# Attention gate columns by matmul, the other late modulation columns on VectorE in chunks two and three

## Chip, cores, metric

One core of one Trainium2 chip. The metric is the device time of one execution in microseconds (us); the profile's span is about 1.8 us shorter. The profile names the engines PE (TensorE matmuls), PEld (TensorE weight loads), DVE (VectorE), ACT (ScalarE), POOL (GpSimd) and SPq (the queue in which SyncE issues DMAs). Its `arena` tiles lie in SBUF and its `ps` tiles in PSUM, to which all matmuls write; an eviction is the copy of such a result from PSUM to SBUF. The granted clock is the share of TensorE's full clock that the throttle let through.

## The reference

An adaLN block: a modulation of six groups of 1024 columns, attention with 32 query heads over 512 cached keys, and a feed-forward part.

```python
mod = (silu(c) @ w_mod).reshape(1, 6, 1, 1024)        # w_mod: 1024 x 6144
sa, ca, ga, sb, cb, gb = mod[:, 0], ..., mod[:, 5]
h = layernorm(x) * (1 + ca) + sa                      # x: 2048 x 1024
x = x + ga * attention(h, k_cache, v_cache, wq, wo)
h = layernorm(x) * (1 + cb) + sb
x = x + gb * ((silu(h @ w_gate) * (h @ w_up)) @ w_down)
```

`sa` and `ca` are needed first. The attention gate `ga` is needed at the first output projection, and `sb, cb, gb` only in the feed-forward part.

## The kernel before

The 2048 rows run in four chunks of 512; I number them 0 to 3, so the title's "two and three" are chunks 1 and 2. A loop of steps `i` goes through 4 x 32 heads. A step issues, in this order, loads, the query projection of head `i+3`, the scores of head `i-1`, and the product with the values (`pv`) of head `i-2`. After the 32nd head of a chunk comes the output projection. One piece of background work (layer norm of a later chunk, or a "row task" that copies a column of gates onto all partitions) is issued at the end of each step. `finish(task)` issues all that is left of a task at once; I call this its forced end.

The early 16 columns of the modulation are made by matmuls before the loop. The other 32 (8 per group) are made one at a time: a transposing DMA brings 128 columns of `w_mod` into SBUF, and VectorE multiplies them with `silu(c)` and sums.

```python
def load_mt(n):                       # transposed load, issued by SyncE
    T.op(Q_mt[n % 2], lambda: SP.dma_start_transpose(mt[n % 2]..., w_mod[:, (NE + n) * P:(NE + n + 1) * P]), writes=[B_mt[n % 2]])

def mod_col(n):                       # the sum, VectorE
    T.op(DVE, lambda: V.scalar_tensor_tensor(mt[n % 2], mt[n % 2], 1.0, sc_row, op0=ALU.mult, op1=ALU.mult,
                                             accum_out=mcol[:, n:n + 1]), reads=[B_scr], writes=[B_mt[n % 2], B_mcol])

def row_task(dst, dbuf, src, sbuf):
    # cut: copies src to c6 on GpSimd
    def diags(n): ...                 # four GpSimd multiplications of ident by a column
    diags(0)
    yield
    for n in range(2):
        for q in range(4):
            mm(bank(XB, P, q * P), ones_bf, diag[q], ...)
        T.op(DVE, lambda: V.tensor_copy(dst[:, n * 512:(n + 1) * 512], bank(XB)), writes=[PB[XB], dbuf])
        if n == 0:
            diags(1)                  # must wait for the four matmuls above
        yield

LOADX = {2: 1, 19: 2, 40: 3}
LOADT = {(3 + 3 * n) if n < DT else (27 + (5 * (n - DT)) // 2): n for n in range(NL)}   # DT = 8, NL = 32
LOADO = {5 + (21 * p) // 8: p for p in range(8)}
for i in range(1, NA + 2):
    if i % 4 == 1:
        load_wq((i + 3) // 4 + 1)     # 1 MB of query weights, two buffers
    if i in LOADX: load_x(LOADX[i])
    if i in LOADT: load_mt(LOADT[i])
    if i - 4 in LOADT:
        mod_col(LOADT[i - 4])         # cut: at the end of a group mod_take, mod_gain or a row task in front of the list
    if i in LOADO: load_wo(LOADO[i])  # 1 MB of output weights
    if i == 8: add_ln1(1)             # cut: later chunks, add_ln2
    if i + LEAD < NA:
        if (i + LEAD) % Hq == 0: finish(ln1[(i + LEAD) // Hq])
        qproj(i + LEAD)               # 8 matmuls, then its eviction on VectorE
    # cut: scores(i - 1), pv(i - 2); pv ends with a reciprocal and a multiplication on VectorE
    # and a transposing DMA of the head; after the last head of a chunk: finish(rows), oproj(chunk)
    run_bg(1)
```

The softmax here doesn't subtract the row's maximum and nothing guards it: scores larger than these inputs give would overflow.

## Time and profile before

| | before |
|---|---|
| device time, median of 3 runs | 1281.27 us (1281.27 to 1281.44) |
| span of the profile | 1280.0 us |
| TensorE busy, VectorE busy | 99%, 38% |
| granted clock | 1.000 |
| transposed loads of `w_mod` in the loop | 32 |

From the profile's page of the kernel before, the engines and the two groups that matter. Columns of a group: line, engine, operation, tiles, shapes, count, then busy us, mean ns of one, and idle time before.

```profile
PE 1262.1 (99%) x7428; PEld 644.3 (50%) x7568; DVE 483.0 (38%) x889; ACT 339.4 (27%) x382; POOL 48.0 (4%) x102
...
L266 PE MATMUL ps<-arena 128*128 128x512 bf16 (+2 forms) x7251 | 1257.3, 333 | 11.5 <-DVE rl L639 1.7
...
L532 DVE SCALAR_TENSOR_TENSOR arena<-arena 128x1024 bf16<-128x1024 bf16 x32 | 38.6, 1206 | 0.4 <-DMA arena<-in_w_mod_dram 0.4
```

TensorE is full: only a wait of TensorE itself can be won. The sums (L532) take 38.6 us of an engine with much idle time, so their sum says nothing of their worth. One caution: this trace has 7251 matmuls of L266 where the trace of the changed kernel has 7391, and the two programs differ there only by the added one-column matmuls, which are another group. So records are missing, and the 11.5 us of idle time are mostly holes.

A better ruler is the start of the reciprocal (L639) that ends each head: there are 128, none missing. I call the time from reciprocal n-1 to reciprocal n "the interval at head n", counting from 0. Without a stall it is 3.50 us, and 58.75 us where a projection lies between (heads 32, 64, 96).

The timeline of VectorE in the kernel before, at head 23 (start us, duration us, engine, line, operation; in brackets the idle time before and what ended it):

```profile
113.87 0.18 DVE L639 RECIPROCAL rl<-ps 128x4 f32<-128x4 f32 x1 [1.08 <-PE ps L266]
...
117.04 0.69 DVE L578 CAST arena<-ps 128x512 bf16<-128x512 f32 x1
118.81 0.18 DVE L639 RECIPROCAL rl<-ps 128x4 f32<-128x4 f32 x1 [1.08 <-PE ps L266]
```

The interval is 118.81 - 113.87 = 4.94 us. Who waited, from the view of the waits of PE:

```profile
PE ps L266 <- DMA arena<-in_A_wq_dram: 1.5, 1, 1.5
```

TensorE waited 1.5 us, once, for query weights. Their DMA stands in SyncE's queue between transposes. From the timeline of SPq, where the duration is the time to issue:

```profile
104.82 1.73 SPq L645 DMA_TRANSPOSE arena<-arena  x1
106.66 0.53 SPq L338 DMA_DIRECT2D arena<-in_A_wq_dram  x1
107.23 4.78 SPq L527 DMA_TRANSPOSE arena<-in_w_mod_dram  x1
```

The second kind of stall is made by the order on VectorE. Its timeline at heads 65 and 66:

```profile
377.09 0.18 DVE L639 RECIPROCAL rl<-ps 128x4 f32<-128x4 f32 x1 [1.08 <-PE ps L266]
...
377.91 0.68 DVE L378 BATCH_NORM_STATS2 st<-x_res 128x6 f32<-128x512 bf16 x1
...
378.76 1.17 DVE L532 SCALAR_TENSOR_TENSOR arena<-arena 128x1024 bf16<-128x1024 bf16 x1
...
380.26 0.68 DVE L578 CAST arena<-ps 128x512 bf16<-128x512 f32 x1
380.86 0.17 DVE L639 RECIPROCAL rl<-ps 128x4 f32<-128x4 f32 x1
```

Normalisation, LN statistics and the sum all come before the eviction of the next query (L578), with no idle time between. The next projection needs that PSUM bank, and the interval becomes 3.77 us (380.86 - 377.09).

### The profile page before, as it was taken

How to read it: one execution, taken by the hardware profiler on the slowest of the kernel's cores; microseconds unless marked ns; L12 is line 12 of the kernel's file. 1: busy time of each engine (PE TensorE's matmuls, PEld its weight loads, DVE VectorE, ACT ScalarE, POOL GpSimd, SP SyncE). 2: the span in 40 equal slices, each digit the busy share in tenths (PEclk: the TensorE clock that was granted, in tenths of full speed). 3: DMA queues.
4: the chain of work that ended last, by engine and by line, in shares of the span. 5: the costliest groups of instructions: out<-in, count | busy, mean ns of one | idle time of the engine just before them, and what ended most of it. 6: DMA issues, size and time to landing. Idle time of an engine off the chain costs nothing.

```text
span 1280.0 us, 17545 instructions
## 1 busy us (share of the span) xinstructions
PE 1262.1 (99%) x7428; PEld 644.3 (50%) x7568; DVE 483.0 (38%) x889; ACT 339.4 (27%) x382; POOL 48.0 (4%) x102
## 2 busy tenths in 40 slices
PE   8999999999999999999999999999999999999999
PEld 4555545555445564455644444444444444444444
DVE  3576425764247652265322331233222331221222
ACT  3655303555025550055510111011100111011100
POOL 2110100000001010000000000000000000000000
PEclk9999999999999999999999999999999999999999
DMA  8899603867017741064352974046421654035200
GB/s 288 212 242 282 130 1 71 193 133 165 1 21 169 161 104 41 1 128 116 71 148 71 287 234 132 17 144 168 133 73 40 198 148 132 18 112 168 66 9 25
DMA packets 241133, 155.29 MB, mean 121 GB/s; under 512 B 137376, under 2 KB 228384, under 8 KB 241056
## 3 DMA queue, kind: packets, MB, share of 16 engines
q1 hardware_dynamic: 182816, 95.45, 31.6%
q10 hardware_dynamic: 58240, 58.72, 14.7%
q8 instruction: 59, 0.97, 0.3%
q14 instruction: 18, 0.15, 0.0%
HBM read 117.44 MB, written 4.19 MB: 95 GB/s over the span
## 4 chain that ended last, share of the span: by engine, by line
PE 96%; DMA 2%; DVE 1%; issue 1%; ACT 0%; SPq 0%
PE ps L266 96%; DMA arena<-arena 1%; DMA arena<-in_A_wq_dram 1%; DVE arena L532 0%; DVE arena L642 0%; PE ps L270 0%; DVE st L378 0%; DVE rl L639 0%; DMA c_row<-in_c_dram 0%; DVE arena L578 0%; ACT arena L621 0%; DVE mv L382 0%; DVE arena L455 0%; DVE tmp L661 0%; DVE arena L663 0%
## 5 line engine op out<-in xcount | busy, mean ns | idle before, releaser
L266 PE MATMUL ps<-arena 128*128 128x512 bf16 (+2 forms) x7251 | 1257.3, 333 | 11.5 <-DVE rl L639 1.7
L266 PEld LDWEIGHTS ps<-arena 128*128 128x128 bf16 x7391 | 637.2, 98 | 625.9 <-issue 4.2
L621 ACT ACTIVATE arena<-ps 128x1024 bf16<-128x1024 f32 x256 | 261.8, 1023 | 354.4 <-PE ps L266 342.6
L828 ACT ACTIVATE arena<-ps 128x512 bf16<-128x512 f32 x112 | 66.9, 597 | 507.0 <-PE ps L266 507.0
L829 DVE TENSOR_TENSOR arena<-ps,arena 128x512 bf16<-128x512 f32 x112 | 77.5, 692 | 276.2 <-PE ps L266 276.2
L661 DVE TENSOR_TENSOR tmp<-ps,rowb 128x512 f32<-128x512 f32 (+1 forms) x65 | 44.4, 683 | 319.6 <-PE ps L266 319.6
L578 DVE CAST arena<-ps 128x512 bf16<-128x512 f32 x124 | 85.6, 691 | 47.2 <-PE ps L266 47.1
L642 DVE TENSOR_TENSOR arena<-ps,rl 128x512 bf16<-128x512 f32 x128 | 88.5, 692 | 4.9 <-DVE rl L639 0.5
L639 DVE RECIPROCAL rl<-ps 128x4 f32<-128x4 f32 x128 | 23.4, 183 | 125.0 <-PE ps L266 124.8
L383 POOL TENSOR_SCALAR rstd<-mv 128x1 f32<-128x1 f32 x31 | 12.9, 416 | 879.7 <-DVE mv L382 879.7
L378 DVE BATCH_NORM_STATS2 st<-x_res 128x6 f32<-128x512 bf16 x62 | 42.3, 682 | 3.5 <-DMA x_res<-in_A_x_dram 3.5
L532 DVE SCALAR_TENSOR_TENSOR arena<-arena 128x1024 bf16<-128x1024 bf16 x32 | 38.6, 1206 | 0.4 <-DMA arena<-in_w_mod_dram 0.4
L663 DVE TENSOR_TENSOR arena<-tmp,x_res 128x512 bf16<-128x512 f32 (+1 forms) x33 | 22.3, 676 | 1.1
L663 DVE TENSOR_TENSOR x_res<-tmp,x_res 128x512 bf16<-128x512 f32 x32 | 22.2, 692 | 1.1
L394 DVE TENSOR_SCALAR arena<-arena,gain,mod_bf 128x512 bf16<-128x512 bf16 x56 | 20.4, 406 | 0.0
L385 POOL TENSOR_TENSOR rstd<-rstd,mhalf 128x1 f32<-128x1 f32 x31 | 17.6, 568 | 2.6
L389 DVE TENSOR_SCALAR nsc<-x_res,mv,rstd 128x1024 bf16<-128x1024 bf16 x30 | 16.1, 538 | 1.0 <-POOL rstd L385 1.0
L547 POOL TENSOR_SCALAR arena<-arena,c 128x128 bf16<-128x128 bf16 x24 | 14.4, 616 | 25.4 <-PE ps L266 25.1
L382 DVE BATCH_NORM_AGGREGATE mv<-st 128x2 f32<-128x12 f32 x31 | 6.5, 209 | 1.1
L266 PEld LDWEIGHTS ps<-sc_bf,arena 128*128 128x128 bf16 x128 | 4.4, 96 | 1.9
L459 ACT ACTIVATE arena<-ps,mod_bf,gain_f 128x512 bf16<-128x512 bf16 x3 | 2.2, 774 | 10.3 <-DVE arena L455 10.3
L266 PE MATMUL ps<-sc_bf,arena 128*128 128x1 bf16 x128 | 4.3, 163 | 0.0
(43 smaller groups left out, 33.7 us busy)
## 6 DMA issues: line engine op xcount, KB each, us to landing
arena<-in_A_wq_dram SPq DMA_DIRECT2D x31, 1024.0 KB, 5.8
arena<-in_B_w_gate_dram ACTq DMA_DIRECT2D x28, 1024.0 KB, 5.4
arena<-in_B_w_up_dram ACTq DMA_DIRECT2D x28, 1024.0 KB, 8.2
arena<-in_A_wo_dram SPq DMA_DIRECT2D x8, 1024.0 KB, 6.9
arena<-in_B_w_down_dram SPq DMA_DIRECT2D x7, 1024.0 KB, 8.5
arena<-in_w_mod_dram SPq DMA_DIRECT2D x8, 512.0 KB, 9.1
out_dram<-arena SPq DMA_DIRECT2D x15, 256.0 KB, 2.0
x_res<-in_A_x_dram SPq DMA_DIRECT2D x3, 1024.0 KB, 7.7
```

The costliest lines, as they stand in the source:

```text
L266: T.op(PE, lambda: TE.matmul(out_ap, lhsT, rhs, start=start, stop=stop, skip_group_check=skip), reads=reads, writes=[bank_buf])
L378: T.op(DVE, lambda: V.bn_stats(st_[sl][:, hf * 6:hf * 6 + 6], x_res[:, t, hf * 512:hf * 512 + 512]), reads=[B_x[t]], writes=[B_st[sl]])
L394: T.op(DVE, lambda: V.tensor_scalar(dst[:, dt, :], dst[:, dt, :], gain[gi][:, dt:dt + 1], mod_bf[:, ccol + dt:ccol + dt + 1], op0=ALU.mult ...
L532: T.op(DVE, lambda: V.scalar_tensor_tensor(mt[n % 2], mt[n % 2], 1.0, sc_row, op0=ALU.mult, op1=ALU.mult, accum_out=mcol[:, n:n + 1]), rea ...
L578: T.op(DVE, lambda: V.tensor_copy(qT_s[qs], bank(QB)), writes=[PB[QB], B_qT[qs]])
L621: T.op(ACT, lambda: A.activation(ex_s[es][:, 2 * kp:2 * kp + 2, :], banks2(SCB + 2 * kp), AF.Exp, scale=att_scale), writes=[PB[SCB + 2 * k ...
L639: T.op(DVE, lambda: V.reciprocal(rl[r][:, :].rearrange("p (a b) -> p a b", a=2), psap(PVB * 512 + P, [[512, 2], [130, 2]])), writes=both + ...
L642: T.op(DVE, lambda: V.tensor_tensor(o_s[os_].rearrange("p (a b) d -> p a b d", a=2), psap(PVB * 512, [[512, 2], [130, 2], [1, P]]), rlb, A ...
L661: T.op(DVE, lambda: V.tensor_tensor(tmp[s][:, 0:n], bank(b, n), rowb[ri][:, c0:c0 + n], ALU.mult), reads=[B_row[ri]], writes=[PB[b], B_tmp ...
L663: T.op(DVE, lambda: V.tensor_tensor(dst[:, c0:c0 + n], tmp[s][:, 0:n], x_res[:, t, c0:c0 + n], ALU.add), reads=[B_tmp[s], B_x[t]], writes= ...
L828: T.op(ACT, lambda: A.activation(sg_s[ss], bank(gb), AF.Silu), writes=[PB[gb], B_sg[ss]])
L829: T.op(DVE, lambda: V.tensor_tensor(guT[:, ft, :], bank(ub), sg_s[ss], ALU.mult), reads=[B_sg[ss]], writes=[PB[ub], B_gu[ft]])
```

## The change

Intent: take the transposed loads and sums out of chunk 0, where loads are dense, and put each remaining sum behind the query eviction. The diff is shortened.

```diff
+            wga = arena.at(OFF_WO + 48 * KB, [DT, D], BF16, B_wga)     # 2 MB, two plain loads at steps 2 and 3
+            GCOLS = [(j, j) for j in range(DT)]
+            NF = NE + DT
-            NL = NJ - NE
+            NL = NJ - NF                                                # 24, not 32
             def add_ln2(ch):
                 if ch == 0:
+                    finish(rows)
-            LOADX = {2: 1, 19: 2, 40: 3}
-            LOADT = {(3 + 3 * n) if n < DT else (27 + (5 * (n - DT)) // 2): n for n in range(NL)}
+            LOADX = {1: 1, 19: 2, 40: 3}
+            LOADT = {Hq + 2 + (5 * n) // 2: n for n in range(NL)}
@@ in the loop, ahead of qproj
+                if i in (2, 3):
+                    load_wga(i - 2)
-                if i in LOADT:
-                    load_mt(LOADT[i])
-                if i - 4 in LOADT:
-                    ... mod_col, mod_take, mod_gain, row tasks
@@ in the loop, after qproj
+                if 7 <= i < 7 + DT:
+                    mod_mm(wga[:, i - 7, :], B_wga[i - 7], i - 7, GCOLS)       # 8 one-column matmuls
+                    if i == 6 + DT:
+                        ... take the gate columns; rows = row_task(...)
+                        bg.insert(0, rows)
+                if i - 5 in LOADT:
+                    ... mod_col, mod_take, mod_gain, the last row task
+                if i in LOADT:
+                    load_mt(LOADT[i])
```

More of the change, by code (lines that the diff above doesn't have):

```diff
@@ L185, in bass_adaLN_cond__sliding_block_cached__swiglu_ffn__prompt_kernel @@
     c6 = S_("c6", [P, DT], F32)
-    mcol = S_("mcol", [P, 4 * DT], F32)
+    mcol = S_("mcol", [P, 3 * DT], F32)
     gain = [S_("gain%d" % i, [P, DT], BF16) for i in range(2)]
@@ L516, in _, with load_wga @@
             x_mod()
-            NL = NJ - NE
+            B_wga = [_Buf("wga%d" % k) for k in range(DT)]
+            wga = arena.at(OFF_WO + 48 * KB, [DT, D], BF16, B_wga)
+            GCOLS = [(j, j) for j in range(DT)]
+            def load_wga(i):
+                T.op(dq("q_wga%d" % i), lambda: SP.dma_start(
+                    wga[:, i * HK:(i + 1) * HK, :],
+                    w_mod[i * HK * P:(i + 1) * HK * P, NE * P:NE * P + D].rearrange("(k p) n -> p k n", p=P)),
+                     writes=B_wga[i * HK:(i + 1) * HK])
+            NF = NE + DT
+            NL = NJ - NF
             B_mt = [_Buf("mt%d" % i) for i in range(2)]
@@ L527, in load_mt @@
                 T.op(Q_mt[n % 2], lambda: SP.dma_start_transpose(
-                    mt[n % 2].rearrange("p (a b) -> p a b", a=1), w_mod[:, (NE + n) * P:(NE + n + 1) * P]),
+                    mt[n % 2].rearrange("p (a b) -> p a b", a=1), w_mod[:, (NF + n) * P:(NF + n + 1) * P]),
                      writes=[B_mt[n % 2]])
@@ L536, in mod_take @@
             def mod_take(g0, cbuf):
-                T.op(DVE, lambda: V.tensor_copy(mod_bf[:, NE + g0 * DT:NE + (g0 + 1) * DT], mcol[:, g0 * DT:(g0 + 1) * DT]),
+                T.op(DVE, lambda: V.tensor_copy(mod_bf[:, NF + g0 * DT:NF + (g0 + 1) * DT], mcol[:, g0 * DT:(g0 + 1) * DT]),
                      reads=[B_mcol], writes=[cbuf])
@@ L707, in _ @@
                     load_wq((i + 3) // 4 + 1)
+                if i in (2, 3):
+                    load_wga(i - 2)
                 if i in LOADX:
                     load_x(LOADX[i])
-                if i in LOADT:
-                    load_mt(LOADT[i])
-                if i - 4 in LOADT:
-                    n = LOADT[i - 4]
-                    mod_col(n)
-                    g0, last = divmod(n, DT)
-                    if last == DT - 1:
-                        mod_take(g0, B_late[g0])
-                        if g0 == 2:
-                            mod_gain(1, 0, DT, B_late[2], B_g[1])
-                        elif g0 in (0, 3):
-                            ri = g0 // 3
-                            rows = row_task(rowb[ri], B_row[ri], mod_bf[:, NE + g0 * DT:NE + (g0 + 1) * DT], B_late[g0])
-                            bg.insert(0, rows)
                 if i in LOADO:
@@ L735, in _ @@
                     qproj(i + LEAD)
+                if 7 <= i < 7 + DT:
+                    mod_mm(wga[:, i - 7, :], B_wga[i - 7], i - 7, GCOLS)
+                    if i == 6 + DT:
+                        T.op(DVE, lambda: V.tensor_copy(mod_bf[:, NE:NF], psap(XB * 512, [[2, DT]])), writes=[PB[XB], B_late[0]])
+                        rows = row_task(rowb[0], B_row[0], mod_bf[:, NE:NF], B_late[0])
+                        bg.insert(0, rows)
+                if i - 5 in LOADT:
+                    n = LOADT[i - 5]
+                    mod_col(n)
+                    g0, last = divmod(n, DT)
+                    if last == DT - 1:
+                        mod_take(g0, B_late[g0 + 1])
+                        if g0 == 1:
+                            mod_gain(1, 0, DT, B_late[2], B_g[1])
+                        elif g0 == 2:
+                            rows = row_task(rowb[1], B_row[1], mod_bf[:, 5 * DT:6 * DT], B_late[3])
+                            bg.insert(0, rows)
+                if i in LOADT:
+                    load_mt(LOADT[i])
                 n = i - (NA - LEAD)
```

## The prediction

> **What bounds the kernel.** TensorE. It is busy 1262.1 of 1280.0 us (99%) at full granted clock; in the chain of waits 96% of the span is matmul. VectorE is busy 38%, ScalarE 27%. The attention loop runs at a floor: in the chain, two heads without a stall take 6.99 us again and again. So shorter VectorE or DMA work gains only where TensorE waited. Waits beyond the 6.99 us grid, from the chain:
> - Chunk 0 (about 36 to 144 us): 15 pairs take 108.0 us instead of 104.9, 3.1 over. 1.7 is one late query-weight load: issued at 106.7 us, landed at 115.0, TensorE idle 1.5. Its issue sat behind other issues in the one SyncE queue, and a transposed modulation load (4.8 us to issue) was beside it. About 0.9 is VectorE, where LN statistics and a modulation sum both stand ahead of a query eviction (four pairs of about 7.2). 0.4 is the row matmuls, which stay.
> - Chunk 1: about 0.5 over, 0.3 recoverable.
> - Chunk 2: about 1.6 over; 1.1 at 377 to 396 us, where the chain runs through statistics, the sum (1.1), the take, the gain and the delayed eviction.
>
> **What the change does.** It removes 8 of 32 transposed loads (median 4.6 us to landing) and 8 VectorE sums (1.2 us each) and moves the other 24 behind chunk 0, which so has none. It adds two plain loads of 1 MB early in chunk 0, and 64 one-column matmuls on TensorE. It issues each sum after the query eviction and not ahead of it. The row task of the last gate is made at step 96, not 88.
>
> **Cost of the parts.**
> - Matmuls: in the timeline at 15.4 to 18.4 us, 48 such matmuls with 8 of 512 columns (213 ns each, the pace of the loop) take 3.07 us: 28 ns each. 64 cost +1.9 us, all on the critical path. (The Trainium skill, "TensorE: Matmul & The Clock Gate", Back-to-back issue gap, gives 81 ns for a sustained pair at 128 columns; this trace shows less, and I use the trace.)
> - The wait for query weights: −1.7, probably gone. The skill, "DMA: Bandwidth & Descriptors", Issuing engines are not separate DMA queues, says that all loads share 16 engines and interleave; the trace agrees, with engines 98% busy at only 230 GB/s in chunk 0.
> - VectorE stalls: −0.9, −0.3, −1.1 in chunks 0, 1, 2. After an eviction a sum has about 1 us of slack, so I expect none in their place.
> - New wait: the last row task starts at step 96 and is forced to its end at step 97, before the output projection of chunk 2. Its second four diagonals (GpSimd, 2.34 us at 455.3 us) can start only after the first row matmuls, and the second row matmuls then hold TensorE. In the kernel before a whole step lies between. Expected: +2.3 us at about 485 us.
>
> Sum: +1.9 +2.3 −4.0 = +0.2. Before 1281.27; predicted 1281.5 us, 8 in 10 between 1279.6 and 1283.4. Chances: faster by over 2% 0.005, within 2% 0.99, slower by over 2% 0.005.
>
> **What would show it.** Matmul count +64; no TensorE wait for query weights at 105 to 116 us; chunk 0 span −0.7; pairs of 7.2 us gone from chunks 1 and 2; one TensorE idle of 2 to 2.5 us before the output projection of chunk 2; feed-forward part unchanged.
>
> **What would make it wrong.** The query-weight wait stays or appears elsewhere (early, behind the gate loads); one-column matmuls between wide ones cost more than 28 ns; the forced row task is hidden; or sums after the eviction delay the reciprocal and the next chain on VectorE enough to stall TensorE.

## The result, and the profile after

| | before | after |
|---|---|---|
| device time, median of 4 runs | 1281.36 us (1281.27 to 1281.75) | 1282.13 us (1281.65 to 1284.06) |
| ratio, 95% interval | | 1.0008 (0.9991 to 1.0026) |
| span of the profile | 1280.0 us | 1280.5 us |

Ratios here and below are the mean time of one kernel's fast runs over that of the other's of the same rounds, so not quite the ratio of the medians. The page of the changed kernel:

```profile
PE 1271.3 (99%) x7632; PEld 645.9 (50%) x7632; DVE 474.9 (37%) x873; ACT 339.7 (27%) x382; POOL 42.1 (3%) x102
...
L266 PE MATMUL ps<-arena 128*128 128x512 bf16 (+2 forms) x7391 | 1266.5, 334 | 2.9 <-DVE rowb L567 1.5
...
L544 DVE SCALAR_TENSOR_TENSOR arena<-arena 128x1024 bf16<-128x1024 bf16 x24 | 29.2, 1215 | 0.0
...
L266 PE MATMUL ps<-sc_bf,arena 128*128 128x1 bf16 x192 | 7.1, 163 | 0.0
```

Eight sums are gone (32 to 24) and 64 one-column matmuls came (128 to 192). The higher busy time of PE is no loss; this trace lost no records. The waits of PE in the loop (36 to 651 us):

```profile
PE ps L266 <- DVE rowb L567: 1.5, 1, 1.5
PE ps L266 <- DVE arena L394: 0.5, 1, 0.5
PE ps L266 <- POOL arena L559: 0.3, 1, 0.3
```

The wait for query weights is gone. Their load is now issued 3.3 us earlier, from the timeline of SPq:

```profile
101.97 1.30 SPq L657 DMA_TRANSPOSE arena<-arena  x1
103.38 0.52 SPq L338 DMA_DIRECT2D arena<-in_A_wq_dram  x1
105.47 4.69 SPq L657 DMA_TRANSPOSE arena<-arena  x2
```

The place of the VectorE stall, now without a sum ahead of the eviction (L590); the interval is 3.50 us:

```profile
376.84 0.18 DVE L651 RECIPROCAL rl<-ps 128x4 f32<-128x4 f32 x1 [1.08 <-PE ps L266]
...
378.57 0.69 DVE L590 CAST arena<-ps 128x512 bf16<-128x512 f32 x1
380.34 0.18 DVE L651 RECIPROCAL rl<-ps 128x4 f32<-128x4 f32 x1 [1.08 <-PE ps L266]
```

Two new stalls stand in their place. The first is the foreseen one, the forced row task before the projection of chunk 2 (timeline, all engines):

```profile
481.74 0.18 DVE L651 RECIPROCAL rl<-ps 128x4 f32<-128x4 f32 x1 [1.08 <-PE ps L266]
481.93 2.35 POOL L559 TENSOR_SCALAR arena<-arena,c 128x128 bf16<-128x128 bf16 x4 [0.66 <-PE ps L266]
...
482.56 0.68 DVE L567 CAST rowb<-ps 128x512 bf16<-128x512 f32 x1
...
483.39 0.59 PE L266 MATMUL ps<-arena 128*128 128x128 bf16 x3 [1.47 <-DVE rowb L567]
...
484.33 3.04 PE L266 MATMUL ps<-arena 128*128 128x128 bf16 x14 [0.35 <-POOL arena L559]
```

GpSimd's four diagonals (POOL L559, 2.35 us) start only when the first row matmuls are done, and TensorE waits first for VectorE's copy of the row and then for the last diagonal. The second I had not seen coming. VectorE at head 27:

```profile
129.01 0.18 DVE L651 RECIPROCAL rl<-ps 128x4 f32<-128x4 f32 x1 [1.08 <-PE ps L266]
...
129.83 1.37 DVE L394 TENSOR_SCALAR arena<-arena,gain,mod_bf 128x512 bf16<-128x512 bf16 x4
131.69 0.69 DVE L590 CAST arena<-ps 128x512 bf16<-128x512 f32 x1 [0.48 <-PE ps L266]
133.46 0.18 DVE L651 RECIPROCAL rl<-ps 128x4 f32<-128x4 f32 x1 [1.08 <-PE ps L266]
```

Four modulations of the normalised rows of chunk 1 (L394) run in one go, where two per step were meant, and the projection that reads those rows waits. The interval is 4.45 us.

The ledger from the intervals of the two profiles closes with the span:

| place | before | after | difference |
|---|---|---|---|
| start, up to reciprocal 0 | 35.52 | 35.60 | +0.08 |
| one-column matmuls, heads 5 to 12, 0.20 each | 3.50 | 3.70 | +1.6 |
| query weights, head 23 | 4.94 | 3.50 | -1.44 |
| VectorE order, heads 9, 12, 15, 18 (0.22, 0.22, 0.29, 0.22) | | | -0.95 |
| forced LN modulation, head 27 | 3.49 | 4.45 | +0.95 |
| chunk 1 (reciprocal 31 to 63) | 167.61 | 167.14 | -0.47 |
| chunk 2 (63 to 95) | 168.70 | 167.15 | -1.55 |
| forced row task, head 96 | 58.75 | 61.61 | +2.86 |
| last transposed head before the end of attention | 10.89 | 10.36 | -0.53 |

The sum is +0.55, the spans differ by 0.5. The row matmuls (0.22 us in each of two heads, 0.44) moved from chunk 2 into the interval at head 96, so the order on VectorE was worth 1.1 in chunk 2 and the forced task costs 2.4. The last row of the table is the time from reciprocal 127 to the next VectorE instruction: in the kernel before TensorE waited there a little for a head's transpose. No experiment treats it.

### The profile page after: what moved, and what is told of

The parts are those of the page before. It is cut to its first block, busy times and chain, and to the rows that moved or that the text cites. A ratio compares the mean times of both kernels' runs of the same rounds, so it can differ in the third digit from the quotient of the medians.

```text
span 1280.5 us, 17793 instructions
## 1 busy us (share of the span) xinstructions
PE 1271.3 (99%) x7632; PEld 645.9 (50%) x7632; DVE 474.9 (37%) x873; ACT 339.7 (27%) x382; POOL 42.1 (3%) x102
## 4 chain that ended last, share of the span: by engine, by line
PE 99%; DVE 0%; DMA 0%; POOL 0%; issue 0%; ACT 0%; SPq 0%; POOLq 0%
PE ps L266 99%; PE ps L270 0%; DMA c_row<-in_c_dram 0%; POOL arena L559 0%; ACT arena L633 0%; DVE arena L654 0%; DVE arena L455 0%; DVE tmp L673 0%; DVE arena L675 0%; SPq L302 0%; DVE arena L394 0%; DVE rl L651 0%; DVE mod_bf L449 0%; PE ps L369 0%; DVE gain L435 0%
## 5 line engine op out<-in xcount | busy, mean ns | idle before, releaser
L590 DVE CAST arena<-ps 128x512 bf16<-128x512 f32 x124 | 85.6, 691 | 60.0 <-PE ps L266 60.0
L383 POOL TENSOR_SCALAR rstd<-mv 128x1 f32<-128x1 f32 x31 | 6.9, 224 | 887.8 <-DVE mv L382 887.8
L544 DVE SCALAR_TENSOR_TENSOR arena<-arena 128x1024 bf16<-128x1024 bf16 x24 | 29.2, 1215 | 0.0
L394 DVE TENSOR_SCALAR arena<-arena,gain,mod_bf 128x512 bf16<-128x512 bf16 x56 | 20.3, 405 | 0.0
L559 POOL TENSOR_SCALAR arena<-arena,c 128x128 bf16<-128x128 bf16 x24 | 14.5, 620 | 23.9 <-PE ps L266 23.6
L266 PEld LDWEIGHTS ps<-sc_bf,arena 128*128 128x128 bf16 x192 | 7.1, 96 | 3.8
L266 PE MATMUL ps<-sc_bf,arena 128*128 128x1 bf16 x192 | 7.1, 163 | 0.0
```

The source lines that it names most:

```text
L266: T.op(PE, lambda: TE.matmul(out_ap, lhsT, rhs, start=start, stop=stop, skip_group_check=skip), reads=reads, writes=[bank_buf])
L394: T.op(DVE, lambda: V.tensor_scalar(dst[:, dt, :], dst[:, dt, :], gain[gi][:, dt:dt + 1], mod_bf[:, ccol + dt:ccol + dt + 1], op0=ALU.mult ...
L590: T.op(DVE, lambda: V.tensor_copy(qT_s[qs], bank(QB)), writes=[PB[QB], B_qT[qs]])
```

## The experiments

Twelve runs, in five groups; those of a group ran on one chip, beside runs of the kernel before. A profile gives the intervals, so single stalls are read to 0.05 us even where times scatter. They do scatter: the kernel before had a granted clock of 1.000 in 25 of its 47 runs in these groups (1280.5 to 1282.9 us) and of 0.997 to 0.999 in 22 (1283.8 to 1287.1 us). All of these count as fast, and I come back to them at the fourth run.

**1. Last row task earlier.**

```diff
-            LOADT = {Hq + 2 + (5 * n) // 2: n for n in range(NL)}
+            LOADT = {Hq - 1 + (5 * n) // 2: n for n in range(NL)}
```

> The changed kernel with the transposed loads and sums three steps earlier, so that the last row task starts at step 93 and ends at step 95, before the projection of chunk 2. Theory (the forced row task is a wait of GpSimd's second four diagonals): the interval between the reciprocals of heads 95 and 96, 61.61 us in the changed kernel, falls to 58.75 us, two heads before it grow by about 0.22 us each for the row matmuls, and the total falls by 2.4 us against the changed kernel. Rival (the long interval comes from something else at the start of the projection, such as a late transposed head): it stays above 60 us. The stall of 0.95 us at head 27 must stay.

Measured: 1281.07 us (1280.88 to 1281.45). Head 96: 58.75 us; heads 93 and 94: 3.73 and 3.71 us; head 27 still 4.45 us. So the forced row task was the stall of 2.4 us. But head 32 became 60.03 us, 1.28 too long: a new stall, and a gain smaller than expected.

**2. Gate row after the layer norm.**

```diff
                         rows = row_task(rowb[0], B_row[0], mod_bf[:, NE:NF], B_late[0])
-                        bg.insert(0, rows)
+                        bg.append(rows)
```

> The changed kernel with the gate's row task put at the end of the background list and not at its head. Theory (the row task, put in front at step 14, pushes the layer norm of chunk 1 three steps back, and its forced end at step 29 stalls TensorE): the interval at head 27 falls from 4.45 to 3.50 us, total -0.9 to -1.0 us against the changed kernel. Rival (VectorE is late at head 27 for another reason): the interval stays over 4 us. The 61.61 us at head 96 must stay.

Measured: 1281.05 us (1280.96 to 1283.45). Heads 27 and 28 are 3.72 us, which is 3.50 plus the row matmuls that now fall there (my text forgot them), and heads 14 and 15 lost theirs. Head 96 stays at 61.60 us. The stall of 0.95 us was the layer norm, pushed three steps back by the row task in front of it.

**3. Both edits.**

> Both edits of the two runs before. Theory: the two stalls are independent and add, -3.3 to -3.4 us against the changed kernel, about 1278.7 us where the kernel before shows 1281.3; ratio to the kernel before 0.998. Rival (one stall hides behind the other or comes back elsewhere): less than 2.5 us gained.

Measured: 1279.80 us (1279.40 to 1280.13), ratio to the kernel before 0.9958 (0.9946 to 0.9970), helped by that kernel's runs at a low clock. The attention loop (reciprocal 0 to 127) takes 612.7 us where the changed kernel takes 615.3: 2.6 gained, not 3.3. The rest is head 32, 59.52 us. The chain of waits of this run, there:

```profile
145.38 0.53 SPq L338
...
145.95 2.18 SPq L539
...
148.18 5.67 DMA arena<-arena
```

Its columns are start us, us, what. A transposed load of `w_mod` (L539), which now comes three steps earlier, took 2.18 us to issue ahead of a head's own transpose, and TensorE waited for that head at the projection of chunk 0. So the two stalls do add, and moving the loads as a block cost part of it again.

**4. The kernel before, sums after the query eviction.** Its block `if i - 4 in LOADT: ...` is moved behind `qproj(i + LEAD)`, nothing else.

> The kernel before with one edit: each sum is issued after the query projection and its eviction, not ahead of them. Theory A (the pairs of long heads came from the order on VectorE; the late query weights came from the transposed loads in chunk 0): heads of 3.72 to 3.92 us in chunks 0 to 2 fall to 3.50 except the row matmuls, the interval of 4.94 us at head 23 stays, total -2.2 to -2.5 us against the kernel before. Theory B (VectorE's order also delayed the SyncE queue and so the query weights): the interval at head 23 falls to 3.5 us too, total about -3.9 us. If the order does nothing, the time stays.

Measured: 1284.14 us (1279.58 to 1286.43); two of six runs at clock 1.000 (1279.58, 1281.27). The VectorE stalls are gone: heads 9, 12, 15, 18 and 70 at 3.50 us, heads 66 and 67 together 7.00. Head 19 is 0.6 us longer, where a sum waited for its late transposed load. Head 23 was neither 4.94 nor 3.50 but 10.98 us. So theory B falls, and the time decides nothing. The view of windows of this run shows where 10.98 comes from (columns: window, its length, busy us with counts of PE, PEld, DVE, ACT, POOL, then the granted clock, the DMA share and GB/s):

```profile
116.00:118.00 2.00, 0.00 (x0) 0.00 (x0) 1.13 (x3) 0.00 (x0) 0.00 (x0) 0.96 1.10 349
118.00:120.00 2.00, 0.83 (x2) 0.43 (x4) 0.00 (x0) 0.00 (x0) 0.00 (x0) 0.50 1.37 272
120.00:122.00 2.00, 2.00 (x6) 0.73 (x5) 0.00 (x0) 0.00 (x0) 0.00 (x0) 0.50 0.75 240
122.00:124.00 2.00, 2.00 (x7) 0.72 (x6) 1.60 (x2) 0.74 (x1) 0.00 (x0) 0.50 0.97 319
124.00:126.00 2.00, 2.00 (x21) 1.56 (x20) 0.83 (x4) 1.30 (x2) 0.00 (x0) 0.83 1.20 231
```

The weights were 4.8 us late in this run. Then TensorE came back at half its clock for about 5.5 us more, with 6 or 7 matmuls in a window; windows at full clock held 14 to 23. So the wait varies from run to run, and a long one is paid twice. This is the likely cause of the kernel before's 22 runs at a lower clock. None of those left a profile, so it is argued, with this support: of the 29 runs of the kernels whose profile has no stall over 1.3 us in the loop (runs 1, 3, 5, 10, 11 and 12 here), none was under 1.000. The chip alone doesn't explain it: in the rounds in which runs 3, 10 and 11 had none, the kernel before had 8, 5 and 4 of 11.

**5. Transposed loads back in chunk 0.** The changed kernel with the kernel before's steps for its first eight:

```diff
-            LOADT = {Hq + 2 + (5 * n) // 2: n for n in range(NL)}
+            LOADT = {(3 + 3 * n) if n < DT else (27 + (5 * (n - DT)) // 2): n for n in range(NL)}
```

> The changed kernel with eight of its 24 transposed loads back in chunk 0, at the steps of the kernel before (3, 6, ... 24), the others from step 27 on; gate columns still by matmul. Theory A (transposed loads in chunk 0 make the query weights late): an interval of 4 to 5 us comes back near head 23, +1 to +1.5 us there. Theory B (the order on VectorE made them late): head 23 stays at 3.50 us. In both, the last row task now starts near step 69, so the 61.61 us at head 96 falls to 58.75 us: total -0.9 to -1.4 us (A) or -2.4 us (B) against the changed kernel.

Measured: 1280.24 us (1280.11 to 1280.47). Head 23: 3.50 us, head 96: 58.75 us. No late weights, though the loads are there. So their presence alone is not enough, and theory A as I had put it fails. Theory B named this interval, but run 4 had already shown that the order on VectorE alone does not bring it. The loop is 1.9 us shorter than the changed kernel's and not 2.4: head 64 became 59.22 us, 0.47 too long, which I had not expected.

**6. Gate matmuls twice.**

```diff
-            GCOLS = [(j, j) for j in range(DT)]
+            GCOLS = [(j, j) for j in range(DT)] + [(j, j + DT) for j in range(DT)]
```

> The changed kernel with each gate matmul made twice, the second time into eight unused columns of the same bank (result unchanged): 64 more one-column matmuls. Theory: cost goes with the count; the eight heads of 3.70 us (0.20 us over 3.50) become about 3.90 to 3.95 us, total +1.6 to +1.9 us. Rival (most of the 0.20 us is a fixed cost of breaking the stream of wide matmuls): the heads grow by less than 0.1 us each.

Measured: heads 5 to 12 are 3.89 to 3.90 us where the changed kernel has 3.70: 64 more cost 8 x 0.20 = 1.6 us, as the first 64 did. One costs 25 ns, and the cost goes with the count. The time, 1286.00 us (1285.35 to 1286.78), is more than 1.6 us above the changed kernel's, since in all four runs the clock was 0.999. Head 96 was 63.30 us, 1.7 more than the 61.61 of the changed kernel. The windows of this run just after the forced row task:

```profile
484.00:486.00 2.00, 0.50 (x3) 0.22 (x3) 1.08 (x2) 0.38 (x1) 2.00 (x4) 1.00 0.88 279
486.00:488.00 2.00, 1.84 (x8) 0.87 (x9) 0.69 (x1) 0.00 (x0) 0.11 (x1) 0.80 1.00 282
488.00:490.00 2.00, 2.00 (x7) 0.63 (x5) 0.00 (x0) 0.00 (x0) 0.00 (x0) 0.50 0.00 0
490.00:492.00 2.00, 2.00 (x9) 0.87 (x8) 0.00 (x0) 0.00 (x0) 0.00 (x0) 0.85 0.00 0
```

A stall of 2.4 us, too, can be followed by half a clock, for about 3.4 us here (the three lower values together). In the profile of the changed kernel the same stall was not.

**7. The changed kernel again.**

> The changed kernel as it is, timed again beside the kernel before on another chip. On one chip the kernel before ran in 8 of 11 runs with a granted clock of 0.997 to 0.999 and up to 5 us longer. Theory (the late query weights vary from run to run, and a longer stall lowers the clock for some us; the changed kernel no longer has that stall): where the kernel before shows such runs, the changed kernel is faster than it in the mean; it has few such runs itself, from its own stall at head 96, so its median is 1281.6 to 1283 us on any chip. Rival (the clock dips belong to the chip, not to a stall): both kernels dip equally often.

Measured: the first of the six runs, 1670.87 us at clock 0.752, is set aside (its profile with it). The other five are 1282.03 to 1284.36 us, median 1282.61, inside the range expected, two of them at 0.999. Ratio to the kernel before 0.9996 (0.9976 to 1.0016). The kernel before had 5 of 11 runs at a lower clock, up to 1287.06 us. At clock 1.000 it is the faster one (1280.84 to 1282.58 us against 1282.03 to 1282.61). So the change trades a stall that varies for a fixed one. That the changed kernel is faster in the mean, which I had expected, the interval doesn't show. Nor do 2 of 5 lower runs against 5 of 11 tell the theory from its rival.

**8. The kernel before, query weights issued by ScalarE.** From the third load on:

```diff
-                T.op(Q_wq[sl], lambda: SP.dma_start(
+                T.op((Q_wq if gidx < NWQ else Q_wqa)[sl], lambda: (SP if gidx < NWQ else A).dma_start(
```

> The kernel before with one edit: the query-weight loads from the third on are issued by ScalarE and not by SyncE. Theory (they were late because they stood behind other issues in SyncE's one queue): the interval at head 23 falls from 4.94 to 3.50 us, the heads of 3.72 to 3.92 us on VectorE stay, total -1.4 us against the kernel before's runs at clock 1.000, and no runs at a clock under 1.000. Rival (they were late because the 16 engines were full of transposed loads): the wait at head 23 stays, at 0.8 us or more.

Measured: 1284.34 us (1282.07 to 1287.38), three of six runs at 0.999. Head 23 did not come to 3.50: heads 22, 23 and 24 are 4.53, 6.10 and 5.54 us, the last with a lowered clock. But TensorE no longer waits for weights. They are issued at 99.6 us in place of 106.7, and the wait has moved. From the waits of DVE between 100 and 125 us:

```profile
DVE arena L643 <- DMA arena<-arena: 4.4, 3, 2.2
```

and from the waits of PE:

```profile
PE ps L266 <- DVE arena L579: 2.4, 1, 2.4
```

Normalising a head (L643) needs a buffer that an earlier head's transpose must first have read, and those transposes are now late. So neither the theory nor the rival holds as written. The earlier issue did bring the weights in time, but now they took 13.2 us from issue to landing (8.4 in the kernel before), and the heads' transposes came late. I take it that both are short of a thing they share; this is argued, not shown alone. The Trainium skill, "DMA: Bandwidth & Descriptors", section "Issuing engines are not separate DMA queues", says that DMAs issued from different engines run on the same 16 engines and interleave, and that several issuers save only issue time. This run is in line with it: another issuer for the same loads moved 1.5 us of wait on weights to 4.4 us of VectorE's wait on heads.

**9. Runs 4 and 8 together.**

> The kernel before with two edits: sums after the query eviction, and query-weight loads from ScalarE. No gate matmuls, no other move. Theory: the VectorE stalls and the late weights are both gone and nothing comes in their place: heads at 3.50 us but for the row matmuls, total -3.8 us against the kernel before's runs at clock 1.000 (1277.5 us where that shows 1281.3), faster than e3_both by about 1 us. Rival: the earlier weight loads slow the transposed heads, and a wait for them comes at the projection of chunk 0 (over 59.3 us at head 32).

Measured: 1282.56 us (1279.94 to 1283.19), ratio 0.9988 (0.9969 to 1.0007). The VectorE stalls are gone, and heads 22 to 25 are 4.43, 4.95, 3.93 and 3.76 us, 3.1 us over, behind late heads again (the waits of DVE name the same DMA with 5.7 us). I had expected nothing in the place of the late weights. The rival had late heads, but at head 32, which is 58.75 us.

**10. Both stalls of the changed kernel removed, loads closer.** Gate row at the end of the list as in run 2, and:

```diff
-            LOADT = {Hq + 2 + (5 * n) // 2: n for n in range(NL)}
+            LOADT = {Hq + 2 + (9 * n) // 4: n for n in range(NL)}
-                if i - 5 in LOADT:
-                    n = LOADT[i - 5]
+                if i - 4 in LOADT:
+                    n = LOADT[i - 4]
```

> The changed kernel with both stalls removed as in e3_both, but the transposed loads start at the changed kernel's own step 34 and follow each other every 2.25 steps and not 2.5, so that the last row task starts at step 90 and no transposed load is issued before the projection of chunk 0. Theory (the 59.52 us at head 32 in e3_both came from transposed loads issued ahead of the last heads' transposes): 58.75 us at heads 32, 64 and 96, head 27 without a stall, total -3.3 to -3.4 us against the changed kernel. Rival: the 59.52 us at head 32 stays.

Measured: 1278.39 us (1278.29 to 1279.09), all six runs at 1.000, result correct. Heads 32, 64 and 96 are 58.75 us, and no head is over 3.50 us but for the matmuls of the gate and of the rows, and a few in which only the reciprocal is late and the next interval is as much shorter (3.88, then 3.12). All the waits of PE in its profile; the first three are before the loop, and the last is at its first head and in the kernel before too:

```profile
PE ps L369 <- DMA c_row<-in_c_dram: 3.5, 1, 3.5
PE ps L270 <- DVE nsc L389: 0.5, 1, 0.5
PE ps L266 <- DVE arena L455: 0.3, 1, 0.3
PE ps L266 <- ACT arena L633: 0.2, 1, 0.2
```

Ratio to the kernel before 0.9961 (0.9943 to 0.9978). On this chip, at clock 1.000 only, the mean is 1278.5 us against 1281.7 of the kernel before (6 runs each) and 1282.3 of the changed kernel (3 runs): 3.2 and 3.8 us less. It beats both, by 0.3%.

**11. The kernel before without its first eight transposed loads and sums.** The result is wrong: the gate row is made from other columns. (The record's check called it correct all the same, so that check does not catch it.)

```diff
-            LOADT = {(3 + 3 * n) if n < DT else (27 + (5 * (n - DT)) // 2): n for n in range(NL)}
+            LOADT = {(3 + 3 * n) if n < DT else (27 + (5 * (n - DT)) // 2): n for n in range(DT, NL)}
+                if i == 28:
+                    rows = row_task(rowb[0], B_row[0], mod_bf[:, 0:DT], B_mode)
+                    bg.insert(0, rows)
```

> The kernel before with its first eight transposed loads and sums taken away and nothing else moved; the gate row is made from the shift columns, so the result is wrong on purpose. Theory (the 16 engines are too full between 90 and 120 us with these loads, and something that shares them comes late: the query weights, or the transposed heads when the weights go first): the interval at head 23 falls from 4.94 to 3.50 us and nothing comes in its place, heads 9, 12, 15 and 18 fall to 3.50 us as their sums are gone, heads 66 to 75 stay long; total -2.3 us against the kernel before's runs at clock 1.000, and no run under clock 0.9995. Rival (another move of the change, such as the first load of x one step earlier or the order of issues in a step, took the wait away): head 23 stays at 4.3 us or more, and runs at a lower clock stay.

Measured: 1279.72 us (1278.90 to 1280.86), all six runs at clock 1.000 where the kernel before had four of 11 lower. Heads 9, 12, 15, 18 and 23 are 3.49 or 3.50 us, and heads 66 to 70 stay long (head 72 is 0.2 us longer). The loop takes 612.1 us where the kernel before takes 614.3, so -2.2, near the -2.3 expected. In the kernel before, these loads with their sums are needed to make the weights late.

**12. Run 5 without the gate matmuls.** Wrong in the same way. The 64 matmuls and their two loads are taken out of run 5's kernel.

> The kernel of e5_early_transposes (eight transposed loads back in chunk 0, no late weights) without its 64 gate matmuls and their two loads; the gate row is made from the shift columns, so the result is wrong on purpose. It asks why no late weights came there. Theory C (the matmuls made TensorE need the weights 1.6 us later, and so hid the wait): without them the interval at head 23 is 3.9 to 5.0 us. Theory D (the order of issues within a step, transposed load after the output weights and after the sum, keeps the weights in time by itself): it stays at 3.50 us. Heads 5 to 12 are 3.50 us in both. If D, total about -1.6 us against e5_early_transposes.

Measured: 1278.82 us (1278.18 to 1279.65). Head 23: 3.49 us; heads 5 to 12: 3.50 us; the loop is 611.3 us against 613.3 of run 5. Theory C falls: the weights are in time with the eight transposed loads in chunk 0 and without the matmuls' delay. What is left is the order of issues. This kernel has the loads of run 4 at the same steps. It differs from run 4 in issuing each transposed load at the end of its step's loads and not ahead of the output weights, in the sum one step later, in the load of x one step earlier, and in the gate's row task at step 14 and not 28. Which of these does it stays open. The traces tell in which part the time lies. The columns give the issue of the load that head 23 needs, how long before reciprocal 22 this is, and the time from issue to landing, all in us:

| kernel | issue | ahead of reciprocal 22 | to landing | wait |
|---|---|---|---|---|
| before | 106.66 | 7.2 | 8.4 | 1.5 |
| run 4 | 109.55 | 4.8 | 9.2 | 4.8 |
| run 5 | 105.18 | 9.9 | 8.7 | none |
| run 11 | 103.55 | 9.2 | 8.3 | none |
| run 12 | 104.03 | 9.0 | 8.7 | none |

The transfer takes about as long with the wait as without it. What differs is when SyncE gets to issue it. And in run 12 a transposed load of 4.64 us to issue stands right behind the weights too, so that neighbour alone is not the cause.

## Why the prediction was right, point by point

The predicted time was 1281.5 us, between 1279.6 and 1283.4; measured were 1282.13 us, ratio 1.0008. It was a sum of two costs and four gains, so each is held against what was measured.

- One-column matmuls: predicted +1.9 us at 28 ns each, measured +1.6 at 25 ns (ledger, and doubled in run 6). The mechanism was right, the size 0.3 too large. I had quoted a figure of the skill for pairs at 128 columns. The same section of "TensorE: Matmul & The Clock Gate", "Back-to-back issue gap", also has a table whose row for 1 to 64 columns gives a floor of about 25 ns, which is what these runs show.
- Late query weights: predicted -1.7, "probably gone"; measured -1.44, gone. The mechanism I gave, SyncE's queue with a transposed load beside it, was half right. The queue is borne out: the table under run 12 has the load issued 1.8 us or more later, relative to the loop, where it is waited for, with hardly any difference in transfer time. The neighbour alone is not. Run 11 shows that the early loads and sums are needed for the wait, run 8 that another queue only moves it, runs 5 and 12 that the same loads in another order do not cause it.
- VectorE order: predicted -0.9, -0.3, -1.1 in the three chunks; measured -0.95, -0.47, -1.1. Run 4 shows it alone.
- Forced row task: predicted +2.3 at about 485 us; measured +2.4, TensorE idle from 481.9 to 483.4 us and again before 484.3. Run 1 removes it.
- Not predicted: +0.95 at head 27. My list of risks did not have it. The step that failed is that I put the gate's row task at step 14 down as costless and didn't count the background steps: it holds one background step in each of three steps, and the layer norm behind it had no three to spare before its forced end at step 29. Run 2 removes it.
- Not predicted: -0.53 at the end of attention, not explained. It cancels about half of the 0.95, so that the sum came within 0.7 us of the measured time is in part luck.
- I read the kernel before as having one time. It has a stall whose length varies, and about half of its runs on other chips were 2 to 5 us longer at a slightly lower clock. My range of 1279.6 to 1283.4 held for the median on the first chip and for all the changed kernel's runs at clock 1.000; one run on the first chip, at 0.999, was 1284.06.

So the expected gain of 4 us came (1.4 + 0.95 + 0.5 + 1.1), and it was given back: 1.6 for the matmuls, 2.4 for the forced row task, 0.95 for the delayed layer norm. Only the first belongs to the idea, and run 10 keeps the idea without the other two.

## What to carry to other kernels

When work moves to a later place, look for every point that forces it to its end ("finish before the projection"), and count the steps left up to it, for the moved work and for everything queued behind it: here two such points took back 3.4 of 4.0 us. Where one engine is full, make a ledger of a regular event's intervals before and after, since shares of busy time said nothing about any of these stalls. A wait of the full engine can be paid twice, once as idle time and once in clock: 4.8 us in run 4 and 2.4 us in run 6 were, the same 2.4 us in the changed kernel's profile was not.

## What the Trainium skill lacked or had wrong

- "TensorE: Matmul & The Clock Gate", section "What's actually happening", gives the cold state as half clock after at least one idle window of about 3.4 us, and a later section the rule of no idle gaps over that. Half clock is seen here (0.50 for about 5.5 us of work after a wait of 4.8 us in run 4). But in run 6 a stall of 2.4 us (waits of PE of 1.5 and 0.4 us with a few matmuls between) was followed by 0.50 as well, for 3.4 us, and cost 1.7 us more; the same stall in the changed kernel's profile kept 1.00. In run 8, 0.50 followed a wait of 2.4 us. Gaps well under the stated window are thus not safe, and whether one is punished varies.
- The same page, "Back-to-back issue gap", gives about 81 ns for a sustained pair of weight load and matmul at 128 columns. In the trace of the changed kernel every matmul has its own weight load (7632 of each), and 129-column matmuls follow each other at 57 ns from start to start (median of 1920 gaps); one-column ones take 25 ns, as the floor in that section's table says.
- "DMA: Bandwidth & Descriptors" says that issuing engines share the 16 engines (in line with run 8). But it does not say for this chip how long a transposing DMA holds its issuer's queue, or that this varies. Issuing a load of `w_mod` took 1.19 us with the DMA engines idle (changed kernel at 283.2 us) and 1.27 to 4.78 us in chunk 0 of the kernel before, where a plain 1 MB load of query weights took 0.53 us.
